# Two pairs' softmax numerators and one pair's x, late in chunk 0: turned by VectorE and carried through DRAM in place of TensorE transposes

## The chip, the cores and the metric

One core of one Trainium2 chip runs the whole kernel. The metric is the device time of one execution in microseconds; the time given is the median of several executions.

## The reference

Two stages. First, causal attention with two sparse masks on q, k, v of shape (8 batches, 8 heads, 576 positions, 64): the first four heads see the last 32 positions, the other four see every 32nd position.

```python
scores = scale * np.matmul(q, k.transpose(0, 1, 3, 2))
mask_local = (rel >= 0) & (rel < stride)
mask_strided = (rel >= 0) & (pos[None, :] % stride == pos[:, None] % stride)
scores = np.where(masks[None, :, :, :], scores, -1000000000.0)
scores = scores - np.max(scores, axis=-1, keepdims=True)
attn = np.exp(scores)
attn = attn / (np.sum(attn, axis=-1, keepdims=True) + 1e-09)
return np.matmul(attn, v).astype(np.float32)
```

Then the heads are joined to x of shape (8, 576, 512), and a feed-forward block is added to it:

```python
xn = (x - mu) / np.sqrt(var + 1e-06) * g_ln
ch = np.maximum(xn @ w_ch1, 0.0) @ w_ch2
return (x + ch).astype(np.float32)
```

The weights arrive as float64 and are cut to float32 inside the kernel.

## The kernel before

**Pairs.** Attention works on pairs of heads: eight batches of four pairs, numbered in the order of work (pair 0 is batch 0, pairs 4 to 7 batch 1, pair 8 the first of batch 2). Even pairs are strided, odd ones local. For a pair the scores of all blocks are made on TensorE (S, line 424), masked and reduced to a row maximum on VectorE (mask, max), the maximum is subtracted on GpSimd (sub, line 489) and the exponential taken on ScalarE (exp, line 496). These numerators must be turned before they can be multiplied with V. Early pairs do it on TensorE into PSUM (PP, line 499: 5 transposes of 128x128 for a local pair, 6 for a strided one) and ScalarE copies the result to SBUF (pt, line 503). Then come the product with V (V, line 519), the division (den, xo), the store of the result to DRAM (st, line 573) and the turn of the result into x, columns first, as the feed-forward stage needs it: again TensorE transposes (X, line 633), ScalarE's high half (xh, line 660) and VectorE's low half (xl, line 665). "High" and "low" are the two parts into which every float32 operand is split for the matmuls.

**The other way.** From pair 9 on the same two turns are made off TensorE. VectorE transposes 32x32 blocks, four DMAs on SP's queue write them to a DRAM tile `pd` (line 605), and loads on ScalarE's queue, one for a local pair and four for a strided one, bring them back with the blocks in their new places (line 618). For x, four DMAs load the stored result with the blocks moved (line 585) and VectorE transposes the 32x32 blocks (line 602). The tile `pt` that the loads fill has one buffer.

**Chunks.** The feed-forward stage takes 512 positions of one batch at a time: chunk 0 for batch 0, and so on to 7; a ninth chunk holds what is left of every batch. For each of 16 blocks f of 128 hidden units there are 12 matmuls for the first layer (8 by w1's high half, F, line 740; 4 by its low half, H, line 752), ScalarE's and VectorE's hh and hl (lines 758 and 763), and 12 matmuls for the second layer (G, line 769). The first layer's PSUM bank has one buffer. From chunk 1 on this is a loop over f, with attention for the batch after next cut into pieces (line 933): a piece's first step, in the chunk's block f = 0, 4, 8, 12, makes the scores of the next pair and the product with V of the present one, between F and H of block f and G of the block before. The first such product is that of pair 8, in block 0 of chunk 1, ahead of G:15 of chunk 0.

**Chunk 0 is written out by hand.** While it runs, the weights are loaded and cut (sc, low, mg, sg on ScalarE and VectorE; byg, add on GpSimd; a column mean cm on TensorE, line 279; cen on VectorE; hi on ScalarE; lo on GpSimd, line 296), and attention for batches 0 and 1 and pair 8's numerators are made. The string ORDER (lines 20 to 56) lists the steps as words, op:number:half:buffer; line 928 issues them in that order, and lines 988 to 997 tie every engine to its order. So a word's place in the string is its place in the queue of every engine that it uses. DMA words go to SP's queue: r (q and k of a later pair, eight DMAs, line 342, into one buffer that tp empties on VectorE), v (V of a later pair, six DMAs for a strided pair, four for a local one, line 387), xr (rows of x for the residual, two DMAs, line 703), st, W. The residual's statistics xs (line 716) end with a power on GpSimd (line 723).

Late in chunk 0 the string runs, with only the words that matter here:

```
before  xo:6 exp:7 cen:13 byg:14 xr:0 hl:12 X:6 F:13 xh:6 xr:1 sub:8 xl:6 H:13 cm:14 G:12 cen:14 xr:2
        hl:13 byg:15 xs:0 PP:7 lo:14:0 F:14 pt:7 tp:9 st:6 add:15 H:14 r:10 cm:15 G:13 cen:15 exp:8 hl:14
        V:7 xr:3 F:15 xo:7 X:7 v:8 H:15 G:14 xh:7 xl:7 v:9 tp:10 PP:8 pt:8 xs:3 st:7 r:11 xs:1
```

Of the kernel before, what the change touches and what calls it, by code (L numbers as in the profile page):

```python
# [20 lines left out]
T:0:0:0 T:0:1:1 c:0:0: c:0:1: T:1:0:2 S:0::0 c:1:0: T:1:1:2 mask:0 max:0 T:2:1:0 c:1:1: sub:0  # L21
S:1::1 c:2:1: exp:0 T:2:0:2 mask:1 max:1 PP:0::0 c:2:0: T:3:0:1 sub:1 pt:0 c:3:0: V:0::2 exp:1
vs:1 S:2::0 den:0 xo:0 PP:1::1 mask:2 X:0::2 pt:1 max:2 W:0 T:3:1:0 xh:0 sub:2 V:1::1 xl:0 c:3:1:
S:3::2 den:1 r:4 xo:1 low:0:0 sc:0:0 low:0:1 exp:2 mg:0:0 mask:3 PP:2::1 X:1::0 pt:2 sg:0:0 W:1
max:3 xh:1 V:2::2 sc:0:1 xl:1 sub:3 tp:4 byg:0 exp:3 W:2 PP:3::0 add:0 den:2 S:4::1 pt:3 mg:0:1
vs:3 xo:2 cm:0::0 low:1:0 X:2::2 W:3 mask:4 sg:0:1 V:3::1 xh:2 max:4 sc:1:0 cen:0 sub:4 xl:2 r:5
hi:0:0 lowA:2:0 mg:1:0 hi:0:1 lo:0:0 F:0 exp:4 den:3 sg:1:0 lowA:3:0 lo:0:1 xo:3 sc:1:1 low:1:1
byg:1 X:3::1 mg:1:1 v:4 sg:1:1 add:1 PP:4::2 xh:3 sc:2:0 xl:3 cm:1::0 mg:2:0 Fb:0 pt:4 lowA:3:1
W:4 cen:1 H:0 lowA:2:1 sg:2:0 hi:1:0 tp:5 byg:2 V:4::0 hh:0 sc:2:1 add:2 hl:0 S:5::1 hi:1:1 st:1
mg:2:1 lo:1:0 cm:2::2 sg:2:1 F:1 W:5 mask:5 sc:3:0 lo:1:1 hi:2:1 cen:2 H:1 mg:3:0 hi:2:0 G:0  # L30
sg:3:0 hh:1 den:4 W:6 sc:3:1 hl:1 lowA:4:1 mg:3:1 lo:2:0 byg:3 lowA:4:0 F:2 sg:3:1 add:3 xo:4
sc:4:0 hi:3:1 W:7 mg:4:0 H:2 lo:2:1 lowA:5:0 sg:4:0 cm:3::0 G:1 cen:3 byg:4 sc:4:1 hi:3:0 mg:4:1
add:4 hh:2 sg:4:1 st:4 hl:2 sc:5:0 X:4::0 lo:3:0 F:3 mg:5:0 xh:4 r:6 lo:3:1 lowA:5:1 xl:4 H:3
sg:5:0 cm:4::0 hh:3 G:2 cen:4 byg:5 sc:5:1 hl:3 lowA:6:1 v:5 add:5 mg:5:1 hi:4:0 sg:5:1 lowA:6:0
lo:4:0 F:4 max:5 sc:6:0 lowA:7:0 mg:6:0 sub:5 lowA:7:1 cm:5::0 sg:6:0 H:4 cen:5 W:8 sc:6:1 byg:6
G:3 hh:4 mg:6:1 add:6 hi:4:1 hl:4 hi:5:0 sg:6:1 lo:5:0 cm:6::0 sc:7:0 F:5 cen:6 W:9 exp:5 lo:4:1
mg:7:0 hi:5:1 sg:7:0 H:5 tp:6 byg:7 sc:7:1 PP:5::0 lowA:8:0 G:4 add:7 st:0 hh:5 hi:6:0 hl:5 lo:5:1
pt:5 r:7 mg:7:1 hi:6:1 S:6::0 lo:6:0 sg:7:1 lowA:9:0 lowA:8:1 F:6 mask:6 sc:8:0 max:6 cm:7::0
mg:8:0 sg:8:0 sub:6 H:6 st:3 G:5 hh:6 cen:7 byg:8 st:2 hl:6 hi:7:0 lo:6:1 tp:7 sc:8:1 hi:7:1
V:5::0 add:8 lowA:9:1 r:8 F:7 mg:8:1 sg:8:1 lo:7:0 den:5 sc:9:0 xo:5 H:7 mg:9:0 sg:9:0 cm:8::0  # L40
hh:7 G:6 exp:6 byg:9 hl:7 W:10 sc:9:1 cen:8 add:9 mg:9:1 hi:8:0 PP:6::0 hi:8:1 sg:9:1 lo:8:0 F:8
tp:8 pt:6 W:11 lo:7:1 hi:9:1 cm:9::0 H:8 lo:8:1 sc:10:0 cen:9 lowA:10:0 G:7 lowA:10:1 mg:10:0 W:12
hi:9:0 sg:10:0 hh:8 byg:10 sc:10:1 hl:8 S:8::0 lowA:11:0 lo:9:0 mg:10:1 F:9 lowA:11:1 sg:10:1 v:6
add:10 mask:8 sc:11:0 H:9 mg:11:0 lo:9:1 lowA:12:1 sg:11:0 cm:10::0 G:8 hh:9 cen:10 byg:11 W:13
# [20 lines left out]
def kernel(  # L65
# [127 lines left out]
    v_l = [v_local(const.tile([P, 4 * NL, D1], F32, name="v_l")),  # L193
           v_local(early.tile([P, 4 * NL, D1], F32, name="v_l1"))]
    v_s = [v_strided(const.tile([P, 2 * NS, D1], F32, name="v_s")),
           v_strided(early.tile([P, 2 * NS, D1], F32, name="v_s1"))]


# [121 lines left out]

    class Pair:
# [43 lines left out]

        def t_rows(self, i, ps):
            ps = ps[:, 0:256 * NA].rearrange("p (a x) -> p a x", a=NA)
            for a in range(NA):
# [434 lines left out]
    for p in first:  # L803
        if p.k in BY_DVE:
            p.load_qk(early.tile([P, 2 * S], F32, name=f"raw{p.id}"))
        elif p.k == 0:
            for i in range(2):
                p.load_rows(i, nc.sync, slice(0, 1))
                p.load_rows(i, nc.scalar, slice(1, 2))
        else:  # L810
            p.load_rows(0, nc.sync)
            p.load_rows(1, nc.scalar)
    nc.sync.dma_start(gcol, g_ln.rearrange("(c p) -> p c", p=P))
    for p in first:
        p.load_v(once=True)

# [211 lines left out]
```

## Time and profile before

| | |
|---|---|
| median of 3 runs | 906.24 us (904.66 to 908.4) |
| profiled execution: span from first to last instruction | 907.3 us |
| profiled execution: time outside the span | none is listed |
| TensorE busy | 884.9 us (98%) |
| VectorE / ScalarE / GpSimd busy | 435.4 / 199.7 / 147.9 us |
| bytes read / written in HBM | 74.02 / 27.72 MB |

The busy time is of the whole span. Chunk 0 ends with G:15 near 160 us; what is changed lies between 126 and 160 us. DMA-issuing instructions are not counted as busy; they are read from the timeline of the queue that issues them, where their length is the time that the issue took, not the transfer.

### The profile page before, as it was taken

The page shows a single profiled execution, that of the slowest core. Times are in us where ns is not written, and L with a number is a line of the kernel's source. Part 1 is how long each engine was busy: PE and PEld are TensorE (multiplying, and loading weights), DVE is VectorE, ACT ScalarE, POOL GpSimd, SP SyncE. Part 2 cuts the span into 40 slices and gives each one's busy share as a digit, 9 for nine tenths or more (in the row PEclk, how much of TensorE's full clock was granted, in tenths as well). Part 3 has the DMA queues.
Part 4 walks back from the last instruction along what each step waited for, and adds up shares of the span by engine and source line. Part 5 has one row for each costly group of instructions (what it writes and reads, how often), then busy time and mean ns, then how long its engine had stood idle before and what let it go on. Part 6 is the DMA issues. An engine that isn't in the chain of part 4 may idle for free.

```text
span 907.3 us, 18531 instructions
## 1 busy us (share of the span) xinstructions
PE 884.9 (98%) x7606; PEld 728.8 (80%) x7606; DVE 435.4 (48%) x864; ACT 199.7 (22%) x326; POOL 147.9 (16%) x186
## 2 busy tenths in 40 slices
PE   7699999999999999999999999999999999999997
PEld 6578787888888888888888888888888888888885
DVE  2888877544654455445644464445533321132113
ACT  3477663111111111111111111111111111111110
POOL 5477774000100011000100010001000000000000
PEclk8999999999999999999999999999999999999999
DMA  8887886675867575766666665757443230002001
GB/s 166 226 257 179 247 196 114 147 111 119 134 142 109 102 137 120 124 91 141 109 134 93 135 104 141 100 127 124 116 85 91 49 128 0 1 1 93 0 1 47
DMA packets 339621, 102.98 MB, mean 114 GB/s; under 512 B 276944, under 2 KB 331344, under 8 KB 339536
## 3 DMA queue, kind: packets, MB, share of 16 engines
q1 hardware_dynamic: 249920, 85.53, 42.9%
q10 hardware_dynamic: 89616, 16.26, 11.5%
q8 instruction: 60, 0.98, 0.5%
q14 instruction: 25, 0.20, 0.1%
HBM read 74.02 MB, written 27.72 MB: 112 GB/s over the span
## 4 chain that ended last, share of the span: by engine, by line
PE 93%; DMA 2%; DVE 1%; issue 1%; SPq 1%; POOL 1%; ACT 0%; DVEq 0%; POOLq 0%; ACTq 0%
PE po L775 42%; PE ph L748 28%; PE ph L755 14%; PE m L515 2%; PE m L445 2%; DMA s<-in_moe_w_ch_dram 1%; PE t L371 1%; PE s L445 1%; DMA rows<-in_q_dram 1%; PE av L515 1%; SPq L351 1%; PE cm L281 1%; PE px L636 0%; PE pp L501 0%; POOL r L270 0%
## 5 line engine op out<-in xcount | busy, mean ns | idle before, releaser
L775 PE MATMUL po<-w,hh 128*128 128x512 f32 x1152 | 359.2, 393 | 0.0
L765 DVE SCALAR_TENSOR_TENSOR hl<-ph,hh 128x512 fp32r<-128x512 f32 x144 | 99.3, 690 | 367.0 <-ACT hh L760 367.0
L775 PEld LDWEIGHTS po<-w,hh 128*128 128x128 f32 x1152 | 213.4, 188 | 44.8
L748 PE MATMUL ph<-xh,w 128*128 128x512 f32 x576 | 226.0, 392 | 1.4 <-ACT w L294 1.2
L775 PE MATMUL po<-w,hl 128*128 128x512 f32 x576 | 224.5, 390 | 0.0
L748 PE MATMUL ph<-xl,w 128*128 128x512 f32 x576 | 224.5, 390 | 0.0
L760 ACT ACTIVATE hh<-ph 128x512 fp32r<-128x512 f32 x144 | 86.1, 598 | 483.7 <-PE ph L755 469.0
L755 PE MATMUL ph<-xh,w 128*128 128x512 f32 x576 | 155.3, 392 | 0.0
L748 PEld LDWEIGHTS ph<-xh,w 128*128 128x128 f32 x576 | 108.3, 188 | 24.1 <-ACT w L294 1.4
L775 PEld LDWEIGHTS po<-w,hl 128*128 128x128 f32 x576 | 108.1, 188 | 23.1
L755 PEld LDWEIGHTS ph<-xh,w 128*128 128x128 f32 x576 | 108.2, 189 | 22.5 <-POOL w L298 0.2
L748 PEld LDWEIGHTS ph<-xl,w 128*128 128x128 f32 x576 | 108.3, 188 | 22.0
L491 POOL TENSOR_TENSOR sm<-sm,mx 128x648 f32<-128x648 f32 (+1 forms) x32 | 40.6, 1269 | 440.4 <-DVE mx L486 440.4
L723 POOL TENSOR_TENSOR rs<-rs,mhalf 128x1 f32<-128x1 f32 x36 | 19.7, 548 | 286.5 <-DVE rs L722 286.5
L497 ACT ACTIVATE sm<-sm 128x648 f32<-128x648 f32 (+1 forms) x32 | 23.8, 742 | 104.3 <-POOL sm L491 104.3
L298 POOL TENSOR_TENSOR w<-r,w 128x512 fp32r<-128x512 f32 x32 | 41.1, 1297 | 7.3 <-ACT w L294 6.9
L687 DVE TENSOR_TENSOR xl<-xo,xh 128x512 fp32r<-128x512 f32 x24 | 16.6, 692 | 38.8 <-ACT xh L686 38.8
L686 ACT ACTIVATE xh<-xo 128x512 fp32r<-128x512 f32 x24 | 15.2, 632 | 62.0 <-DMA pd<-sm 18.2
L486 DVE TENSOR_REDUCE mx<-sm 128x12 f32<-128x648 f32 (+1 forms) x32 | 26.3, 822 | 2.1
L565 DVE TENSOR_TENSOR xo<-m,den 64x64 f32<-64x64 f32 (+3 forms) x120 | 27.1, 289 | 0.0
L781 DVE SCALAR_TENSOR_TENSOR x<-po,rs,x 128x512 f32<-128x512 f32 x36 | 24.5, 737 | 2.0 <-PE po L775 1.8
L718 DVE BATCH_NORM_STATS2 st<-x 128x6 f32<-128x512 f32 x36 | 24.3, 674 | 0.0
(95 smaller groups left out, 561.0 us busy)
## 6 DMA issues: line engine op xcount, KB each, us to landing
s<-in_moe_w_ch_dram SPq DMA_DIRECT2D x32, 512.0 KB
out_dram<-x SPq DMA_DIRECT2D x32, 256.0 KB
raw<-in_q_dram SPq DMA_DIRECT2D x112, 72.0 KB
raw<-in_k_dram SPq DMA_DIRECT2D x112, 72.0 KB
xds<-xo SPq DMA_DIRECT2D x32, 162.0 KB
v_l<-in_v_dram SPq DMA_DIRECT2D x32, 144.0 KB
pd<-sm SPq DMA_DIRECT2D x44, 96.0 KB
pt<-pd ACTq DMA_DIRECT2D x44, 96.0 KB
```

Source lines behind the costliest of these rows:

```text
L298: nc.gpsimd.tensor_tensor(out=t[:, 1], in0=self.w[i], in1=t[:, 0].bitcast(F32), op=ALU.subtract)
L445: nc.tensor.matmul(o, lhsT, rhs, start=True, stop=True, tile_position=(64 * h, pos))
L486: nc.vector.reduce_max(mx[:, :, 0:nt], sm, axis=AX.X)
L491: nc.gpsimd.tensor_tensor(out=sm, in0=sm, in1=mx[:, :, 0:nt].unsqueeze(3).broadcast_to([P, 2, nt, sm.shape[3]]), op=ALU.subtract)
L515: nc.tensor.matmul(at(h, t)[m * j:m * (j + 1)], self.p_cols(rows, t, j), self.v[rows, n, 0:w], start=True, stop=True, tile_position=(64 * ...
L565: nc.vector.tensor_tensor(out=xo[r, t0:t1, h0:h1].rearrange("p t h d -> p h t d"), in0=av, in1=den[r, h0:h1, t0:t1].unsqueeze(3).broadcast_to(
L748: nc.tensor.matmul(ph, w1h[:, cc], x[:, cc, :], start=(new and n == 0 and i == 0), stop=False)
L755: nc.tensor.matmul(ph, w1l[:, cc], xt[c][0][:, cc, :], start=False, stop=(cc == NCC - 1))
L760: nc.scalar.activation(out=hh, in_=ph, func=AF.Relu)
L765: nc.vector.scalar_tensor_tensor(out=hl, in0=ph, scalar=0.0, in1=hh.bitcast(F32), op0=ALU.max, op1=ALU.subtract)
L775: nc.tensor.matmul(po[i], hx[:, cs], w, start=(f == 0 and n == 0), stop=(f == NFC - 1 and n == 2))
L781: nc.vector.scalar_tensor_tensor(out=x, in0=po[i], scalar=rs, in1=x, op0=ALU.mult, op1=ALU.add)
```

## The change

X:6, PP:7, pt:7, PP:8 and pt:8 leave the string. Pair 7's numerators are turned by VectorE and written to DRAM in pT:7, pair 8's in pT:8; pL:7 and pL:8 load them back, on SP's queue and not on ScalarE's. pT:7 writes its blocks to a tile in `pt`'s buffer (own=True), pT:8 to the spare numerator tile. Pair 6's x is loaded turned by blocks in xr2:6 (four DMAs on SP) and finished by VectorE in xT:6; xh:6 and xl:6 then read it from SBUF, one instruction each. st:6 moves ahead of xr:0. The string after, with the same choice of words:

```
after   xo:6 st:6 exp:7 cen:13 pT:7:1 byg:14 xr:0 xr2:6 hl:12 F:13 xr:1 sub:8 H:13 pL:7 cm:14 G:12 cen:14 xr:2
        hl:13 byg:15 xs:0 xT:6 xh:6 lo:14:0 F:14 tp:9 xl:6 add:15 H:14 r:10 cm:15 G:13 cen:15 exp:8 hl:14 pT:8
        V:7 pL:8 xr:3 F:15 xo:7 X:7 v:8 H:15 G:14 xh:7 xl:7 v:9 tp:10 xs:3 st:7 r:11 xs:1
```

The other edits rewrite how steps are called: the loads, memsets and V of the first four pairs become words at the head of the string (vm, R, g, v), in the sequence in which they stood, and several helpers take their engine or copy function as an argument. Where no word of the string ends in D, and none does, that argument is the engine of before.

```diff
-            nc.vector.transpose(xT, self.xraw)
-            split_x(xh[:, cc, :], xl[:, cc, :], xT)
-
-        def p_turned(self):
+            nc.vector.transpose(xT, self.xraw)
+            cc = self.h0 // 2
+            self.xp = [(xT, *(x[:, cc, :] for x in x_t(self.b)))]
...
+        def p_turned(self, own=False):
             nt = self.nt
-            turned = sms[1 - int(self.local)].rearrange("p t h x -> p (t h x)")[
-                :, 0:P * nt].rearrange("p (b t e) -> p b t e", b=4, e=32)
+            if own:
+                turned = smp.tile([P, NS, P], F32, tag="pt", name=f"turned{self.id}").rearrange(
+                    "p t x -> p (t x)")
+            else:
+                turned = sms[1 - int(self.local)].rearrange("p t h x -> p (t h x)")
+            turned = turned[:, 0:P * nt].rearrange("p (b t e) -> p b t e", b=4, e=32)
             nc.vector.transpose(
...
-        def p_load(self):
+        def p_load(self, dma=nc.scalar.dma_start):
...
+        elif op == "pT":
+            p.p_turned(bool(i))
+        elif op == "pL":
+            p.p_load(nc.sync.dma_start)
+        elif op == "xr2":
+            p.x_raw(nc.sync)
+        elif op == "xT":
+            p.x_turned()
```

## Rows read from the trace of the kernel before

**Rows 1.** The page: span, and busy time of each engine.

```profile
span 907.3 us, 18531 instructions
...
PE 884.9 (98%) x7606; PEld 728.8 (80%) x7606; DVE 435.4 (48%) x864; ACT 199.7 (22%) x326; POOL 147.9 (16%) x186
```

**Rows 2.** Busy time by stretch: PE, PEld, DVE, ACT, POOL, clock, DMA share, GB/s.

```profile
126.00:158.00 32.00, 31.95 (x335) 25.73 (x334) 22.98 (x44) 13.53 (x24) 17.16 (x19) 1.00 0.59 119
```

**Rows 3.** The chain of waits from 128 to 158 us: start, length, engine, line.

```profile
131.60 0.66 PE px L636 x6
...
135.00 0.31 PE cm L281 x2
...
138.30 0.37 POOL rs L723
...
141.41 0.49 PE cm L281 x2
...
151.90 0.66 PE pp L501 x6
...
156.19 0.84 PE m L515 x44
```

**Rows 4.** Timeline of VectorE: start, length, instruction, idle before it and releaser.

```profile
129.47 0.68 DVE L765 SCALAR_TENSOR_TENSOR hl<-ph,hh 128x512 fp32r<-128x512 f32 x1
...
138.15 0.78 DVE L415 STREAM_TRANSPOSE qt_l<-raw 128x576 f32<-128x576 f32 x1
...
141.94 0.69 DVE L284 TENSOR_TENSOR r<-r,cm 128x512 f32<-128x512 f32 x1 [2.35 <-PE cm L281]
...
165.26 0.79 DVE L610 STREAM_TRANSPOSE sm<-sm 128x640 f32<-128x640 f32 x1
...
171.44 0.71 DVE L602 STREAM_TRANSPOSE xo<-xraw 128x512 f32<-128x512 f32 x1 [1.84 <-DMA xraw<-xds]
...
189.01 0.92 DVE L610 STREAM_TRANSPOSE sm<-sm 128x768 f32<-128x768 f32 x1
...
217.05 0.70 DVE L602 STREAM_TRANSPOSE xo<-xraw 128x512 f32<-128x512 f32 x1
```

**Rows 5.** Timeline of SP's DMA queue: start, length of the issue, transfer.

```profile
139.62 1.94 SPq L351 DMA_DIRECT2D raw<-in_q_dram  x4
...
143.82 0.44 SPq L711 DMA_DIRECT2D x<-xdl  x1
...
144.93 3.29 SPq L401 DMA_DIRECT2D v_s<-in_v_dram  x6
...
167.86 2.71 SPq L614 DMA_DIRECT2D pd<-sm  x4
...
189.99 1.76 SPq L614 DMA_DIRECT2D pd<-sm  x4
```

**Rows 6.** Timeline of ScalarE and its DMA queue.

```profile
164.79 2.62 ACTq L594 DMA_DIRECT2D xraw<-xds  x4
...
172.58 0.35 ACTq L623 DMA_DIRECT2D pt<-pd  x1
...
173.72 0.60 ACT L760 ACTIVATE hh<-ph 128x512 fp32r<-128x512 f32 x1
...
192.09 2.42 ACTq L628 DMA_DIRECT2D pt<-pd  x4
...
211.66 2.91 ACTq L594 DMA_DIRECT2D xraw<-xds  x4
```

**Rows 7.** Busy time by stretch, columns as in rows 2.

```profile
13.00:16.00 3.00, 0.19 (x9) 0.03 (x2) 0.00 (x0) 1.47 (x2) 0.61 (x1) 0.82 0.51 92
16.00:21.00 5.00, 4.72 (x72) 4.00 (x74) 1.76 (x3) 1.45 (x2) 1.66 (x2) 0.50 0.71 144
30.00:33.00 3.00, 0.20 (x17) 0.05 (x5) 2.05 (x4) 0.00 (x0) 0.00 (x0) 1.00 0.86 250
33.00:38.00 5.00, 2.69 (x64) 2.21 (x64) 4.55 (x7) 2.58 (x4) 2.19 (x2) 1.00 1.04 379
```

More of the change, by code (lines that the diff above doesn't have):

```diff
@@ L20 @@
 ORDER = """
[L21 to L44, printed above, removed]
@@ L59 @@
-ONCE = False
+vm R:0:0 R:0:1 R:1:0 R:1:1:1 R:2:0 R:2:1:1 R:3:0 R:3:1:1 g:0 v:0 v:1 v:2 v:3 T:0:0:0 T:0:1:1 c:0:0:
+c:0:1: T:1:0:2 S:0::0 c:1:0: T:1:1:2 mask:0 max:0 T:2:1:0 c:1:1: sub:0 S:1::1 c:2:1: exp:0 T:2:0:2
+mask:1 max:1 PP:0::0 c:2:0: T:3:0:1 sub:1 pt:0 c:3:0: V:0::2 exp:1 vs:1 S:2::0 den:0 xo:0 PP:1::1
+mask:2 X:0::2 pt:1 max:2 W:0 T:3:1:0 xh:0 sub:2 V:1::1 xl:0 c:3:1: S:3::2 den:1 r:4 xo:1 low:0:0
+sc:0:0 low:0:1 exp:2 mg:0:0 mask:3 PP:2::1 X:1::0 pt:2 sg:0:0 W:1 max:3 xh:1 V:2::2 sc:0:1 xl:1
@@ new lines @@
+sub:3 tp:4 byg:0 exp:3 W:2 PP:3::0 add:0 den:2 S:4::1 pt:3 mg:0:1 vs:3 xo:2 cm:0::0 low:1:0 X:2::2
+W:3 mask:4 sg:0:1 V:3::1 xh:2 max:4 sc:1:0 cen:0 sub:4 xl:2 r:5 hi:0:0 lowA:2:0 mg:1:0 hi:0:1 lo:0:0
+F:0 exp:4 den:3 sg:1:0 lowA:3:0 lo:0:1 xo:3 sc:1:1 low:1:1 byg:1 X:3::1 mg:1:1 v:4 sg:1:1 add:1
+PP:4::2 xh:3 sc:2:0 xl:3 cm:1::0 mg:2:0 Fb:0 pt:4 lowA:3:1 W:4 cen:1 H:0 lowA:2:1 sg:2:0 hi:1:0 tp:5
+byg:2 V:4::0 hh:0 sc:2:1 add:2 hl:0 S:5::1 hi:1:1 st:1 mg:2:1 lo:1:0 cm:2::2 sg:2:1 F:1 W:5 mask:5
@@ new lines @@
+cm:6::0 sc:7:0 F:5 cen:6 W:9 exp:5 lo:4:1 mg:7:0 hi:5:1 sg:7:0 H:5 tp:6 byg:7 sc:7:1 PP:5::0
+lowA:8:0 G:4 add:7 st:0 hh:5 hi:6:0 hl:5 lo:5:1 pt:5 r:7 mg:7:1 hi:6:1 S:6::0 lo:6:0 sg:7:1 lowA:9:0
+lowA:8:1 F:6 mask:6 sc:8:0 max:6 cm:7::0 mg:8:0 sg:8:0 sub:6 H:6 st:3 G:5 hh:6 cen:7 byg:8 st:2 hl:6
+hi:7:0 lo:6:1 tp:7 sc:8:1 hi:7:1 V:5::0 add:8 lowA:9:1 r:8 F:7 mg:8:1 sg:8:1 lo:7:0 den:5 sc:9:0
+xo:5 H:7 mg:9:0 sg:9:0 cm:8::0 hh:7 G:6 exp:6 byg:9 hl:7 W:10 sc:9:1 cen:8 add:9 mg:9:1 hi:8:0
+PP:6::0 hi:8:1 sg:9:1 lo:8:0 F:8 tp:8 pt:6 W:11 lo:7:1 hi:9:1 cm:9::0 H:8 lo:8:1 sc:10:0 cen:9
@@ new lines @@
+lo:11:1 sc:13:1 xl:5 lowA:14:1 hl:11 sub:7 hi:12:1 mg:13:1 V:6::0 lowA:14:0 r:9 byg:13 F:12 sg:13:1
+den:6 add:13 xo:6 st:6 sc:14:0 H:12 lo:12:1 lowA:15:0 mg:14:0 exp:7 cm:13::0 sg:14:0 G:11 hi:13:1
+cen:13 pT:7:1 byg:14 xr:0 xr2:6 hh:12 sc:14:1 hl:12 lo:13:1 hi:13:0 mg:14:1 lo:13:0 sg:14:1 F:13
+add:14 xr:1 sc:15:0 H:13 sub:8 pL:7 mg:15:0 cm:14::0 hh:13 G:12 cen:14 xr:2 sg:15:0 hi:14:0 hl:13
+byg:15 xs:0 xT:6 xh:6 lo:14:0 F:14 tp:9 xl:6 lowA:15:1 add:15 sc:15:1 H:14 r:10 cm:15::0 hh:14 G:13
+cen:15 exp:8 hl:14 pT:8 hi:14:1 mg:15:1 hi:15:0 sg:15:1 lo:15:0 V:7::0 hi:15:1 pL:8 xr:3 F:15
@@ L191, in v_strided, with v_frames @@
         return t
[L193 to L196, printed above, removed]
+    v_l = [const.tile([P, 4 * NL, D1], F32, name="v_l"),
+           early.tile([P, 4 * NL, D1], F32, name="v_l1")]
+    v_s = [const.tile([P, 2 * NS, D1], F32, name="v_s"),
+           early.tile([P, 2 * NS, D1], F32, name="v_s1")]
+    def v_frames():
+        for t in v_l:
+            v_local(t)
+        for t in v_s:
+            v_strided(t)
     sms = [const.tile([P, NS, 2, 64], F32, name=f"sm{i}") for i in range(2)]
@@ L358, in load_rows @@
             if self.rows is None:
-                self.rows = early.tile([CT, 2, 2, NA, 2, D], F32, name=f"rows{self.id}")
+                self.rows = early.tile([CT, 2, 2, NA, CC, D], F32, name=f"rows{self.id}")
             src = (q, k)[i]
@@ L368, in t_rows @@
             for a in range(NA):
-                for c in range(2):
+                for c in range(CC):
                     for h in range(2):
@@ L658, in x_parts, with x_high @@
             return [(src, dst(xh), dst(xl)) for src, dst in parts]
-        def x_high(self, px):
-            self.xp = self.x_parts(px)
+        def x_high(self, px=None):
+            if px is not None:
+                self.xp = self.x_parts(px)
             for src, hi, _ in self.xp:
@@ L802 @@
     first = pairs[0:NHP]
[L803 to L815, printed above, removed]
     NP = len(pairs)
@@ L843, in one @@
         p = pairs[k]
-        if op == "T":
+        eng, copy = nc.gpsimd, nc.scalar.copy
+        if op.endswith("D"):
+            op, eng, copy = op[0:-1], nc.vector, nc.vector.tensor_copy
+        if op == "R":
+            if k == 0:
+                p.load_rows(i, nc.sync, slice(0, 1))
+                p.load_rows(i, nc.scalar, slice(1, 2))
+            else:
+                p.load_rows(i, nc.scalar if buf else nc.sync)
+        elif op == "vm":
+            v_frames()
+        elif op == "Z":
+            t = room(f"d{len(ps)}", buf - 1) if buf else wake
+            for _ in range(k):
+                nc.tensor.matmul(
+                    t[:, 0:2 * P].rearrange("p (n x) -> p n x", x=P), mean,
+                    mean.unsqueeze(1).broadcast_to([P, 2, P]), start=True, stop=True)
+        elif op == "g":
+            nc.sync.dma_start(gcol, g_ln.rearrange("(c p) -> p c", p=P))
+        elif op == "T":
             p.t_rows(i, room(f"t{k}{i}", buf))
         elif op == "c":
-            p.t_copy(i)
+            p.t_copy(i, copy)
         elif op == "S":
```

90 lines of the change are left out of this document (46 added, 44 removed).

## The prediction

> **What bounds the kernel now.** I read the page's busy times first: TensorE is busy for 884.9 of 907.3 us [rows 1], so only time on TensorE, or time in which it is made to wait, can matter. The stretch table confirms this for the place of the change: from 126 to 158 us TensorE is busy for 31.95 of 32.00 us at full clock, VectorE for 22.98, ScalarE for 13.53 [rows 2]. Then I read the chain of waits there [rows 3]. It is TensorE nearly throughout, with one excursion: between the column mean of block 14 (135.00) and that of block 15 (141.41) it leaves TensorE and runs over VectorE and GpSimd. After VectorE's sign step for block 15 (line 264) come GpSimd's power for the first residual (line 723, 138.30), its low half of w1 for block 14 (line 298) and the block sums, and the next column mean waits for those. What TensorE does inside that excursion is not what ends it.
>
> **What is removed.** X:6, PP:7 and PP:8 are 6, 5 and 6 transposes. On the chain six take 0.66 us (X:6 at 131.60, PP:8 at 151.90) [rows 3], so five take 0.55. The 1.87 us do not all come back: PP:7 lies inside the excursion, is absent from the chain, and without it TensorE would only come earlier to a column mean that GpSimd has not fed yet. So X:6 moves the excursion's start by 0.66, PP:7 gives nothing (at most its 0.55), PP:8 gives 0.66: **1.32 us**, bounds 1.32 and 1.87. ScalarE's two evacuations of PP go, and xh:6 becomes one instruction; ScalarE was idle for more than half of the stretch, so this is costed at nothing.
>
> **What is added on VectorE.** Transposes like pT:7 and pT:8 take 0.79 and 0.92 us later in this kernel, one like xT:6 0.71 [rows 4]: 2.42 us into a stretch with 9 us free. Place by place: pT:7 stands ahead of hl:12, which ran from 129.47 for 0.68 us [rows 4]; it would end at 130.9 instead of 130.15, and its waiter F:13 can now start at 131.60, so this is covered with 0.7 us to spare. xT:6 stands ahead of tp:9 and cen:15; there VectorE waited 2.35 us for TensorE [rows 4], which covers it. pT:8 delays only the steps of w2's block 15, used after the next chunk's first block. If xr2:6 is late, the cover before cen:15 is used up first, and then TensorE waits.
>
> **What is added on SP.** This is the term that decides. The queue issues in order, and the change puts on it four writes for pT:7, four for pT:8, four loads for xr2:6, one for pL:7 and four for pL:8; st:6 goes out earlier, ahead of xr:0, xr:1 and xr:2 and of r:10.
> The first part is covered. st:6 is out before pT:7 ends at 130.3, since xo:6 precedes pT:7 on VectorE. pT:7's writes then need 1.76 us (as at 189.99 [rows 5]), so xr:0 leaves near 132.1; with 1.1 us of issue and 2.5 of landing, both as below, it is there by 135.7. Line 723, which takes the statistics made from it, is due 0.66 earlier than 138.30, at 137.6. xr2:6 leaves at 133.2, needs 2.6 to 2.9 us of issue [rows 6] and a landing of 0.3 to 2.5, xT:6 0.71 more, and tp:9 twice 0.78 [rows 4]: tp:9 ends before 139.6, as now, or up to 1.2 us later. r:10 waits for tp:9 and left at 139.62 [rows 5]; I take 0.3 late, since the quick landing is the nearer in a window with little traffic. pL:7 leaves SP ahead of r:10, and V:7 stands behind cm:15 and a whole FFN2 block, so pair 7's detour is free.
> Pair 8's is not. r:10's eight loads took 4.2 us to issue (139.62 to 143.82), so pT:8's writes start at 144.1 and take 1.76 (2.71 at worst): 145.9 [rows 5]. pL:8 must see them landed. The same hop later took 0.34 us (191.75 to 192.09) and, behind the output stores, 2.0 (170.57 to 172.58) [rows 5, 6]; I take 1.0, nearer the first, since no output store is in flight here: 146.9. Its four loads need 2.42 [rows 6]: 149.3. **Behind them on SP stand xr:3 (1.11 us) and v:8 (3.29)** [rows 5], so v:8 is fully issued at 153.7 instead of 148.2. Landing: a later xraw issued by 214.57 was used at 217.05 without a wait, so 2.48 is enough in the quiet; one issued by 167.41 was waited for until 171.44, so 4.03 when crowded [rows 4, 6]. Against the hop's 0.34 I take 1.7, and v:8 is there at 155.4.
> The blocks of V for pair 8 start at 156.19 on the chain [rows 3]; with 1.32 us gained they could start at 154.87. TensorE therefore waits **0.5 us**. With every low end v:8 lands at 153.1 and nothing is lost; with every high end at 160.6, and 5.7 us are lost. pL:8's own data is there before v:8's.
>
> Here a rule of the Trainium skill speaks another way. The rows show SP needing about 0.52 us per raw load [rows 5], so that 17 added transfers weigh by their issue. "DMA: Bandwidth & Descriptors", section "Issuing engines are not separate DMA queues", says that using several issuers saves only the issuing time, usually small relative to the transfer itself. By that rule the order on SP would hardly matter, the wait would be nil and the sum 1.32 us.
>
> **After that.** v:9, st:7 and r:11 follow late on SP, and pair 9's writes (167.86) with them. ScalarE's load of pair 9 waits for those writes (172.58), and the next hh (173.72) is queued behind it [rows 5, 6]; a late hh holds the PSUM bank that TensorE's next block needs. Bounds: nothing, and the lateness that is left by then, some 2 us. I take 0.2, because SP has pauses before it in which to catch up.
> **At no cost:** loads, memsets and V of the first four pairs, now words of ORDER in the same sequence; the engine arguments, which keep their old values; the turned tile and pt sharing a buffer, since pL:7 must wait for those writes anyway, and the other reader that pL:8 waits for, V:7, stands two FFN1 blocks ahead of the V blocks of pair 8.
>
> **Sum.** -1.32 + 0.5 + 0.2 = -0.6 us. The profiled execution's span is 907.3; of its time outside the span nothing is listed, and it lies 1.1 above the median of the runs, 906.24, inside their range. 906.7 against that span is **905.6** against the median.
>
> **The rivals.**
> *Nothing is late (904.9).* The transfers land as fast as the quickest rows, v:8 before 154.87, and 1.32 us remain (904.4 if the excursion shortens by PP:7 too). For: the DMA engines are little loaded in this window compared with later. Against: seven steps in a row on one queue must each be quick. The queue rule named above, taken at its word, gives this case.
> *The V loads become the wait (907 to 911).* Place: TensorE at pair 8's V blocks. It decides against the change from the point where v:8 lands after 156.2, only 0.8 us beyond my middle. Price: 157.5 gives 906.24 - 1.32 + 2.6 + 0.5 of knock-on = 908.0. With some 3 us of standing there is also the clock: TensorE stood 2.8 of the 3 us from 13 to 16 and the granted clock was half (1.2 GHz) from 16 to 21; it stood 2.8 of those from 30 to 33, and the clock stayed full (2.4 GHz) from 33 to 38 [rows 7]. Five microseconds at half clock lose 2.5 us of work, which carries this case to 911. For: the pessimistic end of every term is a row of this trace.
> "VectorE: DVE Perf Modes", section "Rules for kernel authors", advises turning a 128x128 block on TensorE where a PSUM destination will do. By that advice this case is the one to expect.
> *It gives back what it saves (906.2).* The transposes go, but the excursion over GpSimd lengthens (the residual xr:0 comes late through SP, so line 723 and the low half behind it do), and cm:15 stays near 141.4. For: the excursion is already the end there. Against: by the times above xr:0 is there 1.9 us before line 723 is due.
>
> **How the numbers follow.** My forecast, a short wait: 0.42. Nothing late: 0.22. V loads late: 0.27. Given back: 0.09. The range 903.7 to 909.3 takes in the first, second and fourth with 0.7 us for the median's own scatter (the runs shown spread over 904.66 to 908.4), and most of the third; some 0.12 stay outside. About half a per cent, 4.5 us, is what a measurement of this kernel can tell from no change. Faster by that needs more than twice all the transposes removed: 0.03. Slower by that needs the third case with the clock's fall: 0.05. Within: 0.92.
>
> **What would show it.** Right: 17 fewer transposes on TensorE after 126 us; cm:15 near 140.7 and still after GpSimd's sums; V's blocks for pair 8 near 155.4, with a short gap ahead and v_s as releaser; pL:8 leaving SP near 146.9 and v:8 done there near 153.7. Wrong: a gap of over 2 us ahead of those blocks, half clock after it, gaps on TensorE in the first four blocks of chunk 1 that ScalarE's hh ends, or cm:15 at 140.2 or earlier, which would mean that PP:7 counted. A change of over 2 us down would mean that I have missed a wait that these transposes caused.

## The result and the profile after

| | before | after |
|---|---|---|
| median of 6 runs each, side by side | 907.59 us (904.66 to 909.99) | 914.81 us (911.44 to 916.56) |
| ratio, 95% interval | | 1.0079 [1.0056, 1.0103]: **slower by 0.8%** |
| profiled execution, span | 907.3 us | 914.8 us |

The time lies outside the range given. The second rival happened: the V loads became the wait.

The page of the kernel after, span and busy times (as [rows 1]):

```profile
span 914.8 us, 18519 instructions
...
PE 885.6 (97%) x7589; PEld 728.8 (80%) x7589; DVE 437.7 (48%) x866; ACT 197.4 (22%) x323; POOL 148.1 (16%) x186
```

TensorE has 17 transposes fewer and is still busy 0.7 us longer than in [rows 1]; its idle time grew from 22.4 to 29.2 us. Where, the stretch table says (as [rows 2]):

```profile
126.00:158.00 32.00, 29.07 (x302) 23.01 (x290) 21.88 (x37) 12.21 (x21) 17.04 (x18) 1.00 0.62 130
158.00:160.00 2.00, 0.32 (x2) 0.19 (x2) 1.64 (x5) 0.00 (x0) 0.55 (x1) 0.92 0.89 179
160.00:166.00 6.00, 5.10 (x51) 4.24 (x52) 5.25 (x16) 0.38 (x1) 1.80 (x2) 0.50 0.96 156
166.00:170.00 4.00, 4.00 (x18) 3.30 (x17) 2.59 (x4) 0.36 (x1) 0.00 (x0) 0.93 0.74 144
```

The first row was 31.95 of 32 busy; now it is 29.07, and from 160 to 166 us the granted clock is 0.50, that is 1.2 of 2.4 GHz. Third, the timeline of TensorE, where the bracket gives the idle time before an instruction and what ended it:

```profile
140.96 1.19 PE L767 MATMUL ph<-xh,w 128*128 128x512 f32 x4 [1.06 <-POOL w L302]
142.52 0.49 PE L285 MATMUL cm<-bsum,mean 128*128 128x128 f32 x2 [0.37 <-POOL bsum L281]
...
155.52 0.97 PE L448 MATMUL m<-kt_l,qt_l 64*32 64x64 f32 x72
159.35 0.32 PE L517 MATMUL m<-v_s,pt 54*64 54x64 f32 x2 [2.85 <-DMA v_s<-in_v_dram]
160.90 1.51 PE L517 MATMUL m<-v_s,pt 54*64 54x64 f32 x42 [1.23 <-DMA v_s<-in_v_dram]
```

In the kernel before TensorE was idle for 0.05 us from 126 to 158 us [rows 2]; now it has two small stops at GpSimd's work (1.06 and 0.37) and then **2.85 and 1.23 us at the first products of pair 8 with V**, both ended by loads of V. Fourth, the chain of waits (as [rows 3]), which says what those loads waited for:

```profile
139.10 0.38 POOL rs L735
...
139.62 1.28 POOL w L302
...
142.52 0.49 PE cm L285 x2
...
148.07 3.85 DMA pd<-sm
...
152.98 0.53 SPq L723
...
154.14 0.49 SPq L404
...
156.53 4.24 DMA v_s<-in_v_dram
...
160.90 1.51 PE m L517 x42
162.41 4.88 PE po L787 x12
```

Read it downwards: GpSimd's power comes at 139.10, 4.16 us after cm:14 (134.94) where it was 3.46 (138.30 in [rows 3], after 134.84), and the column mean behind it at 142.52; the writes of pT:8 land (148.07 to 151.92), pL:8 can finish, xr:3 follows at 152.98, v:8 at 154.14, and the last V load needs 4.24 us to land. G:15 then takes 4.88 us at 162.41, part of it at half clock; in the kernel before it took 2.9 us, from 156.96 to 159.86. The same on SP's queue (as [rows 5]):

```profile
131.12 1.76 SPq L625 DMA_DIRECT2D pd<-turned  x4
132.97 0.40 SPq L723 DMA_DIRECT2D x<-xdl  x1
...
134.17 2.81 SPq L596 DMA_DIRECT2D xraw<-xds  x4
...
141.20 3.64 SPq L356 DMA_DIRECT2D raw<-in_q_dram  x4
144.89 2.12 SPq L356 DMA_DIRECT2D raw<-in_k_dram  x4
147.11 1.89 SPq L625 DMA_DIRECT2D pd<-sm  x4
149.14 3.79 SPq L639 DMA_DIRECT2D pt<-pd  x4
152.98 0.53 SPq L723 DMA_DIRECT2D x<-xdl  x1
...
154.14 3.24 SPq L404 DMA_DIRECT2D v_s<-in_v_dram  x6
```

and on VectorE (as [rows 4]), which has a wait that the prediction did not name, for xr:3, at 158.25:

```profile
130.25 0.84 DVE L621 STREAM_TRANSPOSE turned<-sm 128x640 f32<-128x640 f32 x1
...
137.93 0.69 DVE L730 BATCH_NORM_STATS2 st<-x 128x6 f32<-128x512 f32 x1 [0.68 <-DMA x<-xds]
...
139.14 0.71 DVE L602 STREAM_TRANSPOSE xo<-xraw 128x512 f32<-128x512 f32 x1
...
144.25 0.97 DVE L621 STREAM_TRANSPOSE sm<-sm 128x768 f32<-128x768 f32 x1
...
158.25 0.69 DVE L730 BATCH_NORM_STATS2 st<-x 128x6 f32<-128x512 f32 x1 [3.91 <-DMA x<-xds]
```

**An account of the 7.5 us.** Executions differ by up to 4.8 us ahead of the change: before any of these words, X:5's first matmul starts between 117.57 and 122.34 us in the fourteen profiled executions of this study. So I compare an inner stretch, from that matmul to the first matmul of block 5 of chunk 1 (where the lateness has settled): 62.15 us before (121.44 to 183.59), 68.63 after (122.23 to 190.86), +6.48. Its parts, from starts on TensorE: X:5 to cm:14 12.71 us, not 13.40 (-0.69); cm:14 to cm:15 7.58, not 6.57 (+1.01); cm:15 to the first layer of block 0 10.19, not 10.90 (-0.71); block 0 of chunk 1 14.42, not 7.55 (**+6.87**); after it no change (23.73 each). Of the 6.87, 4.08 are the two stops; the other 2.79 are put down to the clock, since the V blocks and G:15 behind the stops run at half of it. The rest of 7.5 is start (0.8) and end (0.2). Block 0's two ends on TensorE, before:

```profile
152.31 0.48 PE L748 MATMUL ph<-xh,w 128*128 128x512 f32 x1
...
159.86 0.39 PE L748 MATMUL ph<-xh,w 128*128 128x512 f32 x1
```

and after:

```profile
152.71 0.39 PE L760 MATMUL ph<-xh,w 128*128 128x512 f32 x1
...
167.13 0.39 PE L760 MATMUL ph<-xh,w 128*128 128x512 f32 x1
```

### The profile page after: what moved, and what is told of

It reads as the page before. It is cut to its first block, busy times and chain, and to the rows that moved or that the text cites. A ratio compares the mean times of both kernels' runs of the same rounds, so it can differ in the third digit from the quotient of the medians.

```text
span 914.8 us, 18519 instructions
## 1 busy us (share of the span) xinstructions
PE 885.6 (97%) x7589; PEld 728.8 (80%) x7589; DVE 437.7 (48%) x866; ACT 197.4 (22%) x323; POOL 148.1 (16%) x186
## 4 chain that ended last, share of the span: by engine, by line
PE 87%; DMA 4%; SPq 3%; issue 2%; DVE 2%; POOL 2%; ACT 0%; DVEq 0%; POOLq 0%
PE po L787 40%; PE ph L760 26%; PE ph L767 13%; PE m L517 2%; PE m L448 2%; DMA s<-in_moe_w_ch_dram 1%; SPq L356 1%; PE t L376 1%; DMA xds<-xo 1%; DMA rows<-in_q_dram 1%; PE s L448 1%; POOL r L274 0%; DMA v_s<-in_v_dram 0%; PE av L517 0%; DMA pd<-sm 0%
```

## The experiments

The theory: pair 8's writes, loads and what stands behind them on SP cost more than all the transposes give. The rivals: pair 7 and x do it, or the residual's rows, or one transfer alone (v:8). The table has every run, each beside runs of the kernel before on the same chip; the last columns are from its profiled execution: the inner stretch, and TensorE's stops of 0.8 us and more in it.

| run | median, before beside it | ratio, 95% interval | stretch (62.15 before) | stops |
|---|---|---|---|---|
| e1_v8_early | 914.46, 907.81 | 1.0077 [1.0055, 1.0099] | 66.38 | 1.21, 1.63, 2.38 |
| e2_busy | 914.03, 907.81 | 1.0070 [1.0050, 1.0090] | 68.25 | none (0.74) |
| e3_pair8_pe | 907.23, 907.81 | 0.9999 [0.9985, 1.0014] | 62.13 | 0.84 |
| e4_xr0_early | 914.52, 907.81 | 1.0075 [1.0055, 1.0095] | 68.17 | 3.30, 1.06 |
| e5_three_early | 911.13, 906.93 | 1.0046 [1.0029, 1.0064] | 64.81 | 1.16, 0.95 |
| e6_busy_short | 912.36, 906.93 | 1.0059 [1.0037, 1.0082] | 66.70 | 1.58 |
| e7_only_pair8 | 910.97, 906.93 | 1.0043 [1.0028, 1.0057] | 65.30 | 1.16, 0.94 |
| e8_pair8_pe_xr0 | 906.45, 906.93 | 1.0000 [0.9987, 1.0012] | 61.75 | none |
| e9_r10_behind | 912.33, 906.91 | 1.0046 [1.0029, 1.0064] | 67.12 | 2.26, 0.91 |
| e10_pL8_act | 910.48, 906.91 | 1.0037 [1.0023, 1.0051] | 65.51 | 1.05, 1.85 |
| e11_tp10_behind | 915.91, 905.93 | 1.0114 [1.0096, 1.0133] | 70.91 | 0.84, 5.18 |
| e12_r10_between | 909.18, 906.53 | 1.0028 [1.0014, 1.0042] | 64.06 | 1.07, 1.06 |

### Which part costs

**e3: pair 8 back on TensorE**, pair 7 and x as in the kernel after.

```diff
-cen:15 exp:8 hl:14 pT:8 hi:14:1 ... hi:15:1 pL:8 xr:3 ... v:9 tp:10 xs:3
+cen:15 exp:8 hl:14 hi:14:1 ... hi:15:1 xr:3 ... v:9 tp:10 PP:8::0 pt:8 xs:3
```

> The changed kernel with pair 8's turn alone put back on TensorE (PP:8, pt:8; no pT:8, no pL:8): pair 7 and pair 6's x stay off TensorE. Theory A: SP loses the 8 transfers that made v:8 late, v:8 is fully issued 5 to 6 us earlier, no wait at the V blocks and no fall of the clock: within 1.5 us of the kernel before, most likely 0 to 0.5 below it, since PP:8's 0.66 us are back and xr:0 is late. Rival (the queue is too late by pair 7 and x alone): a wait of over 1 us remains at the V blocks.

The time is that of before. Both stops at V are gone, and on SP v:8 leaves at 145.04, which is 25.9 us after X:5's start (119.11); it was 23.5 in the kernel before (144.93 in [rows 5]) and 31.9 in the kernel after. SP's timeline of e3:

```profile
145.04 3.43 SPq L404 DMA_DIRECT2D v_s<-in_v_dram  x6
```

So all of the loss comes with pair 8. **e7** is the opposite, the order of before with pair 8's detour alone (in the code of the kernel after, with its rewritten calls):

```diff
-cen:15 exp:8 hl:14 hi:14:1 ... hi:15:1 xr:3 ... v:9 tp:10 PP:8::0 pt:8 xs:3
+cen:15 exp:8 hl:14 pT:8 hi:14:1 ... hi:15:1 pL:8 xr:3 ... v:9 tp:10 xs:3
```

> The kernel before with pair 8's turn alone taken off TensorE (pT:8, pL:8 on SP); X:6 and PP:7 stay on TensorE, st:6 and xr:0 where they were. Theory: pair 8's eight transfers alone make v:8 and xr:3 late; without pair 7's and x's transfers r:10 is not late, so the wait is a little shorter than the 4.1 us of the changed kernel: 2 to 4 us, and the clock may fall; 2 to 7 us above before. Rival (the loss needs all three parts together, because each uses up some slack): under 1.5 us above before.

TensorE's timeline of e7 has the stop at V again, shorter:

```profile
153.50 0.29 PE L516 MATMUL m<-v_s,pt 54*64 54x64 f32 x2 [1.16 <-DMA v_s<-in_v_dram]
154.73 0.98 PE L516 MATMUL m<-v_s,pt 54*64 54x64 f32 x42 [0.94 <-DMA v_s<-in_v_dram]
```

Alone it costs some 4 us by the medians (3.15 in the stretch). Pair 7 and x cost nothing by themselves (e3), but they make r:10, and all behind it, later: r:10 leaves 19.0 us after X:5's start in the kernel after and 18.2 in e7, and its issue takes 5.8 us against 4.1. The same detour then costs 7. **e4** and **e8** move xr:0 ahead of st:6, in the kernel after and in e3:

```diff
-xo:6 st:6 ... byg:14 xr:0 xr2:6
+xo:6 xr:0 st:6 ... byg:14 xr2:6
```

> The changed kernel with xr:0 ahead of st:6 and of pT:7's writes on SP. Theory: the stretch between cm:14 and cm:15 became longer because xr:0 landed late (VectorE waited 0.68 us for it, GpSimd's power came later, and TensorE stood 1.06 us at H:14 and 0.37 at cm:15). With xr:0 early these two gaps shrink to 0.6 us or less in sum, cm:15 comes 0.6 to 1.0 us earlier against cm:14, r:10 leaves SP earlier by the same, and the wait at the V blocks shrinks with it: the time falls by 0.5 to 2 us, still 5 to 7 above before. Rival (GpSimd's own work sets that stretch): the gaps stay over 1 us and nothing moves.

> The changed kernel with pair 8 back on TensorE and xr:0 ahead of st:6. Theory: X:6 and PP:7 are worth at most 1.2 us and half of that was lost because xr:0 came late; with xr:0 early the stretch from cm:14 to cm:15 shrinks from 7.4 to 6.8 us: 0.3 to 1.5 us below the kernel before, which at the scatter of the runs may or may not show. Rival: GpSimd's chain holds cm:15 anyway, and the time stays within 0.3 us of before.

cm:14 to cm:15 shortens from 7.58 to 6.82 in e4, and from 7.37 in e3 to 6.82 in e8. So the late residual rows did lengthen the excursion, by 0.55 to 0.76 us. e4's time did not move: the stop at V took up what was gained. e8 is 0.40 below before in the stretch and level in the ratio: the transposes of pair 7 and x are worth nothing that can be measured.

### What the stop costs beside its length

**e2 and e6** keep TensorE at work while it would wait: 30 and 16 matmuls of 128x128 into a part of PSUM that nothing reads, ahead of pair 8's V blocks, added to the kernel's work.

```diff
+        if p.k == 2 * NHP:
+            for _ in range(30):
+                nc.tensor.matmul(ps[:, 1408:1536], mean, mean, start=True, stop=True)
         av = p.v_blocks(ps)
```

> The changed kernel with 30 matmuls of 128x128, 3.3 us, added on TensorE between the scores of pair 9 and pair 8's V blocks, into unused PSUM columns; their result is not read. Theory A: v:8 lands when it did, so the V blocks start as late as before (near 160.9), but TensorE has been at work meanwhile, the granted clock stays full, and the 2.5 us lost at half clock come back: about 4.5 to 5 us above the kernel before instead of 7.2. Rival: the fall of the clock is not tied to that wait, or costs nothing beyond it; then the time stays near 7 us above before.

> The changed kernel with 16 added matmuls ahead of pair 8's V blocks instead of 30. The 30 took 6.96 us, 0.23 each, not the 3.3 meant, and so covered the whole wait and more; 16 take 3.7. Theory: the V blocks start when v:8 has landed, some 4.2 us after the scores of pair 9, with under 1 us of standing; the clock stays full; the time is 4 to 5 us above the kernel before, 2 to 3 below the changed one. Rival (the clock falls for another reason or the half-clock stretch costs nothing): 7 us above before.

TensorE's timeline of e2, the added matmuls and the V blocks behind them:

```profile
151.83 6.96 PE L690 MATMUL m<-mean 128*128 128x128 f32 x60
158.72 0.91 PE L517 MATMUL m<-v_s,pt 54*64 54x64 f32 x44
```

Thirty took 6.96 us, twice what I had assumed, so e2 only swaps the loss for the added work. Sixteen took 3.84, nearly as long as the stops (4.08). TensorE's timeline of e6:

```profile
152.29 3.84 PE L690 MATMUL m<-mean 128*128 128x128 f32 x32
```

There is no stop at V, the clock is 1.00 from 146 to 190 us, and block 0 of chunk 1 takes 11.20 us instead of 14.42, no more than its 7.55 of before and the added work. So in this trace the 2.79 us are gone together with the stops, which bears out that they are the price of the clock's fall. The medians alone do not show it: the loss is 5.4 us against the before beside it, where after's is 7.2, but the intervals overlap, and the trace is that of e6's fastest execution (910.09, median 912.36; its own excursion was 0.5 longer than after's). The other 4 us remain, now as added work.

### Is it one late transfer?

**e1** moves v:8 ahead of st:6, long before pair 8's writes.

```diff
-xo:6 st:6 ... X:7 v:8 H:15
+xo:6 v:8 st:6 ... X:7 H:15
```

> The changed kernel with one word moved: v:8 goes out on SP ahead of st:6, where SP stood idle, and no longer behind pL:8 and xr:3. Theory A (TensorE waits for v:8 alone, which SP issues too late, and the clock falls because of that wait): TensorE stands at pair 8's V blocks for at most 1 us instead of 4.1, the half-clock stretch behind it is gone, and the time is 6 to 7 us below the changed kernel, within 1.5 us of the kernel before. Theory B (pair 8's numerators come late through DRAM as well, so that pL:8 is the wait as soon as v:8 is not): TensorE still stands 2 to 4 us, released by the load of pt, and the time stays 3 to 7 us above before.

The V blocks start without a wait, and the time stays. Two other stops have come, one at the first layer and one at the second, in TensorE's timeline of e1:

```profile
159.06 0.50 PE L759 MATMUL ph<-xh,w 128*128 128x512 f32 x1 [1.63 <-DVE hl L776]
...
164.48 0.70 PE L786 MATMUL po<-w,hh 128*128 128x512 f32 x2 [2.38 <-DVE x L792]
```

Both are VectorE's doing, which stands for xr:3 and has hl and the residual's last step queued behind that wait (VectorE's timeline of e1):

```profile
156.31 0.70 DVE L729 BATCH_NORM_STATS2 st<-x 128x6 f32<-128x512 f32 x1 [4.82 <-DMA x<-xds]
```

So xr:3 was late at the same time as v:8, in parallel; curing one of them alone did not lower the median. **e5** moves all three loads that suffered: xr:0 and v:8 ahead of st:6, xr:3 ahead of r:10.

```diff
-xo:6 st:6 ... byg:14 xr:0 xr2:6 ... H:14 r:10 ... pL:8 xr:3 ... X:7 v:8 H:15
+xo:6 xr:0 v:8 st:6 ... byg:14 xr2:6 ... H:14 xr:3 r:10 ... pL:8 ... X:7 H:15
```

> The changed kernel with three words moved on SP: xr:0 and v:8 ahead of st:6, xr:3 ahead of r:10, so that nothing that is due early in chunk 1 stands behind pL:8. Theory (SP is a queue in which v:8 and xr:3, each alone, come late enough to stop TensorE: v:8 directly, xr:3 through VectorE's statistics, behind which hl and the last step of chunk 0 stand; with v:8 alone moved the second stopped it for 1.6 and 2.4 us): no gap over 0.5 us on TensorE from 145 to 170 us, full clock, time 0.5 to 2 us below the kernel before. Rival (pair 8's numerators are themselves late once v:8 and xr:3 are not, or take the DMA engines from them): a gap of 1 to 4 us ahead of pair 8's V blocks released by the load of pt, and 2 to 6 us above before.

About half of the loss went. Now the releaser at the V blocks is pair 8's own data; r:10's issue took 8.3 us ahead of its writes (140.08 to 148.40). TensorE's timeline of e5:

```profile
155.59 0.81 PE L516 MATMUL m<-v_s,pt 54*64 54x64 f32 x40 [1.16 <-DMA pt<-pd]
...
163.01 0.70 PE L786 MATMUL po<-w,hh 128*128 128x512 f32 x2 [0.95 <-DVE x L792]
```

**e9** puts r:10 behind pL:8 and st:7, and tp:10 at the string's end; **e11** then moves tp:10 and r:11 into the loop behind G:15; **e12** is e9 with r:10 between pair 8's writes and its loads.

```diff
 e5:  xr:3 r:10 ... pT:8 ... pL:8 ... xo:7 ... v:9 tp:10 xs:3 st:7 r:11 xs:1
+e9:  xr:3 ... pT:8 ... pL:8 ... xo:7 st:7 r:10 ... v:9 xs:3 xs:1 tp:10 r:11
+e11: xr:3 ... pT:8 ... pL:8 ... xo:7 st:7 r:10 ... v:9 xs:3 xs:1 ... G:15 tp:10 r:11
+e12: xr:3 ... pT:8 ... r:10 pL:8 ... xo:7 st:7 ... v:9 xs:3 xs:1 tp:10 r:11
```

> The run e5_three_early with r:10 (eight loads) moved behind pL:8 and st:7 on SP, and tp:10 moved to the string's end. Theory: all of the loss is pair 8's chain standing in one queue, and in e5 the last piece of it was r:10, 8.3 us ahead of pT:8's writes. Then those writes leave SP right after pT:8 (near 145), pL:8 is issued by about 151 instead of 152.9 and landed by about 154, the gap ahead of pair 8's V blocks is under 0.5 us, the later stop at G:15 of e5 (0.95) goes with st:7 earlier, the clock stays full, and the time is 905.5 to 907 (ratio 0.9985 to 1.000). Rival: a chain VectorE, DRAM, loads of about 10 us cannot be fitted between exp:8 and the V blocks in whatever order, since what it waits for is landings and not its place: then pL:8's data again comes after 154.5, TensorE waits 1 us or more with pt as the releaser, and the time is 909 or more. A second rival: r:10 and tp:10 are now late for pair 10's scores, a new gap after 180 us.

> The run e9_r10_behind with tp:10 and r:11 moved behind G:15, out of VectorE's queue ahead of the first block's hl of chunk 1. Theory: e9 showed that the detour fits between exp:8 and pair 8's V blocks when nothing stands ahead of it on SP, and that what was left of the loss is tp:10, 5.9 us of waiting for r:10, ahead of hl. With tp:10 behind G:15 that hl runs near 157, neither the next first-layer block nor G:15 waits, the gaps of TensorE from 140 to 170 sum to under 1.5 us, and the time is 905.5 to 907.5 (ratio 0.9985 to 1.0005): level with before, since the 1.3 us removed are less than what a measurement tells apart. Rival: the lateness only moves on once more; r:11 and the writes of pair 9 come later, and a gap of 2 us or more with a DMA, ScalarE's hh or VectorE's hl behind it appears between 165 and 200 us, and the time stays at 909 or more.

> The run e9_r10_behind with r:10 one place earlier: on SP behind pT:8's writes and ahead of pL:8, so between the two runs e5 (r:10 ahead of the writes) and e9 (behind the loads). tp:10 stays at the string's end. Theory: pair 8's detour and r:10 together have about 10 us of SP's time between pT:8 (near 142) and pair 8's V blocks (near 154) and fit only in this order, since r:10's issue fills the time in which pT:8's writes land. Then the writes leave by 144, r:10 by 148.5, pL:8 by 152 and is landed near 154; tp:10 waits for r:10 under 1 us; the gaps of TensorE from 150 to 170 sum to under 1.5 us, and the time is 906 to 908 (ratio 0.999 to 1.002), better than e5 and e9 (1.0046 each). Rival: there is no order in which all three are in time; pL:8 is then 1 to 2 us late as in e5 or the stop at hl comes back as in e9, gaps sum to 2 us or more, and the time is 909 or more.

In e9 pair 8's data is in time: its writes leave at 142.96 and its loads at 145.63. But VectorE waits 3.35 and 2.52 us for r:10 in tp:10, with the next hl behind it; the second rival had the right transfer and the wrong victim, hl and not pair 10's scores. VectorE's timeline of e9:

```profile
154.47 1.26 DVE L422 STREAM_TRANSPOSE qt_s<-raw 128x576 f32<-128x576 f32 x1 [3.35 <-DMA raw<-in_q_dram]
158.26 1.26 DVE L422 STREAM_TRANSPOSE kt_s<-raw 128x576 f32<-128x576 f32 x1 [2.52 <-DMA raw<-in_k_dram]
```

and TensorE's, with both stops:

```profile
160.09 0.79 PE L759 MATMUL ph<-xh,w 128*128 128x512 f32 x1 [2.26 <-DVE hl L776]
...
165.46 0.71 PE L786 MATMUL po<-w,hh 128*128 128x512 f32 x2 [0.91 <-DVE x L792]
```

In e11 the wait has moved on to r:11: VectorE waits 5.88 us for it in tp:11, again ahead of an hl, and the longest stop of the study follows, with the clock down to 0.53 from 175 to 180 us. The rival was right. VectorE's timeline of e11:

```profile
171.03 0.78 DVE L417 STREAM_TRANSPOSE qt_l<-raw 128x576 f32<-128x576 f32 x1 [5.88 <-DMA raw<-in_q_dram]
```

and TensorE's:

```profile
174.25 0.80 PE L759 MATMUL ph<-xh,w 128*128 128x512 f32 x1 [5.18 <-DVE hl L776]
```

e12 has the lowest median of the orders tried and still loses: pL:8 is late by 1.07, and a later block waits 1.06 for hl. Theory and rival each had part of it; no order tried had everything in time. TensorE's timeline of e12:

```profile
156.19 0.81 PE L516 MATMUL m<-v_s,pt 54*64 54x64 f32 x40 [1.07 <-DMA pt<-pd]
...
177.49 0.50 PE L759 MATMUL ph<-xh,w 128*128 128x512 f32 x1 [1.06 <-DVE hl L776]
```

**e10** leaves the order and moves pL:8 alone to ScalarE's queue.

```diff
-            p.p_load(nc.sync.dma_start)
+            p.p_load(nc.scalar.dma_start if k == 8 else nc.sync.dma_start)
```

> The kernel after, with pL:8 alone on ScalarE's queue instead of SP's, as pairs from 9 on have it. Theory: what is late on SP is what stands behind the pL:8 that waits for its own writes. Then xr:3 and v:8 leave SP 3.8 us and more earlier (v:8 issued by about 153.5 instead of 157.4, landed near 157), the wait ahead of pair 8's V blocks falls from 4.1 to about 1 to 2 us, the clock's fall goes, and the time is near 910. Rival: the wait only changes queues: pL:8 now holds ScalarE until pT:8 is landed (near 152), and hh:15 behind it holds the first layer's PSUM bank, so a gap of 2 us or more appears ahead of the next first-layer block or G:15 with ScalarE as the releaser, and the time stays at 913 or more.

The time is the theory's and the mechanism the rival's: ScalarE stands at pL:8 until 153.3, hh:15 is behind it, and the stop is now ahead of chunk 1's first layer, where it hides the late V loads (v:8 was still issued only by 156.98). ScalarE's timeline of e10, with its DMA queue:

```profile
149.79 3.52 ACTq L639 DMA_DIRECT2D pt<-pd  x4
153.35 0.60 ACT L772 ACTIVATE hh<-ph 128x512 fp32r<-128x512 f32 x1 [6.11 <-DMA x<-xdl]
```

and TensorE's:

```profile
154.73 0.50 PE L760 MATMUL ph<-xh,w 128*128 128x512 f32 x1 [1.85 <-DVE hl L777]
```

What follows from all twelve: the cost lies in pair 8's detour and in no single transfer of it. Between exp:8 and the V blocks SP has to issue r:10, pair 8's eight transfers, xr:3, v:8 and st:7, each with a consumer that stands in some engine's order ahead of work that TensorE needs. No run with the detour had all of them in time, and no run was faster than the kernel before by more than the scatter. Whether another buffer for raw, which would let r:10 leave earlier, would do it was not tried.

## Why the prediction was wrong

**Right.** X:6 and PP:8 gave 0.69 and 0.71, forecast 0.66 each; PP:7 gave nothing; VectorE's transposes took 0.84, 0.97 and 0.71 us, and TensorE waited for none of them; nothing was lost after block 0, where I had taken 0.2. The place of the loss, v_s as its releaser and half clock behind it were named as the signs of the second rival.

**The step that failed is the wait at pair 8's V blocks, forecast 0.5 us, measured 4.08.** The profiled execution of the kernel after is 0.8 us late already at X:5, so I take 0.8 off its times before I compare them with the forecast. Then v:8 was there at 160.0 and not at 155.4, 4.6 us late. Two mis-sized terms make most of it, the landing of v:8 and the issue of r:10; the links in order:

- r:10 left at 140.4, not 139.9 (+0.5): VectorE waited 0.68 us for xr:0, ahead of xT:6 and tp:9.
- r:10's issue took 5.81 us, not 4.2 (+1.6). I had given this term no range.
- From the last issue of pT:8's writes to the end of pL:8's issue it took 3.9 us, not 1.0 and 2.42 (+0.5). One write landed 3.85 us after its own issue began; pL:8's issue overlapped the landing.
- v:8 landed 3.4 us after its issue, not 1.7 (+1.7).
- The issue of pT:8's writes, of xr:3 and of v:8 went as forecast (+0.3 with the pauses between).

TensorE came to the blocks at 155.7, not 154.87, since the excursion grew; that took 0.8 off the wait.

The largest of these terms could have been read in the trace of the kernel before. There the last of v:8's loads was issued by 148.22 and landed, by its semaphore's records, at 151.53: 3.3 us, and 3.3 in e3 too. So v:8 did not land more slowly behind the detour; I had priced its landing by other transfers. One of those was misread: 0.34 us (191.75 to 192.09) is not the time in which four writes land. The loads of that row left between 192.1 and 193.8, each behind its own write, and the last write landed at 193.27, 1.5 us after its issue. Nor was the window quiet: the DMA share was 0.59 in [rows 2], and 0.63 and 0.69 in the next two stretches of 32 us. With 3.3 in place of 1.7 my own sum has v:8 at 157.0 and a wait of 2.1 us, which is the second rival; its chance of 0.27 was too small. That the sum of my high ends, 160.6, lies near 160.0 is luck: it has 4.2 for r:10's issue and 2.71 for that of pT:8's writes, which took 5.81 and 1.89.

**The clock was in the rival and not in the forecast:** 2.79 us by the account above, 2.5 named there. Even that rival's upper end, 911, is 4.8 above its 906.24, and the medians differ by 7.2. "Slower by over 0.5%" deserved far more than 0.05.

**xr:0 through SP was rejected too firmly.** I counted 1.9 us in hand. With 0.8 taken off, xr:0 left at 132.2, as forecast, but VectorE had its rows at 137.1, not 135.7: they landed 3.8 us after their issue, where I had taken 2.5. The excursion grew by 1.01, of which e4 gave back 0.76. So the third rival happened too, inside the larger loss.

**Not seen at all:** the second late consumer, xr:3 on VectorE, which e1 uncovered.

The rule quoted from the Trainium skill, "DMA: Bandwidth & Descriptors", section "Issuing engines are not separate DMA queues", would have given no loss from the order on SP. e10, which changes the issuing queue of four transfers and nothing else, halves the loss (1.0079 to 1.0037), so the measurement decides against using it that way. The advice of the Trainium skill, "VectorE: DVE Perf Modes", section "Rules for kernel authors", to turn such blocks on TensorE, agrees with e3 (ratio 0.9999 with pair 8 turned there).

## What to carry to other kernels

Price a detour through DRAM by its whole chain (issue, landing of the writes, issue, landing of the loads) and by the deadline of everything queued behind it. Where the trace has the landing of the very transfer, take that and not another's. Here 0.71 us of TensorE's time was exchanged for a chain of about 10 us (144.25 to 152.93 and a landing) with no slack. If each reordering only hands the wait to the next transfer, that speaks for putting the step back. Compare stretches inside the span when the start scatters by more than the effect.

## What the runs showed of the hardware that was not expected

A stop of TensorE is paid twice only sometimes. In the profiled executions half clock followed stops of 2.85 and 1.23 (after), 3.30 and 1.06 (e4), 1.16 and 0.94 (e7), 1.85 (e10), 2.26 (e9) and 5.18 us (e11), but not those of 1.63 and 2.38 (e1) or 1.16 and 0.95 (e5), nor 1.07 and 1.06 (e12). e1's profiled execution was its second fastest (911.77, median 914.46), so others of its executions may have fallen; what decides it is left open. A 128x128 float32 matmul of the added ones took 0.23 us (6.96 for 30, which the trace shows as 60 instructions), where six transposes of the same size took 0.66 in [rows 3]. The six loads of v:8 landed 3.3 to 3.4 us after their last issue without the detour ahead of them (before, e3, e8) and 2.6 to 3.6 with it (after, e2, e4, e6, e7, e10). Issuing the same eight loads of r:10 took from 4.1 us (e7, 136.55 to 140.67) to 8.3 us (e5).
